# Batch 0 of an FFT filter with MLP: small columns on Pool, earlier angles, one filter copy and the last evacuation on ScalarE

## The chip, the cores and the metric

The kernel runs on one core of one Trainium2 chip. The metric is the device time of one execution in microseconds (us); lower is better. The kernel before took 772.74 us, the median of three runs from 772.51 to 773.15.

## The reference, cut to what matters

```python
X = np.fft.rfft(x, axis=1)                      # x: 8 batches x 3008 x 256
Y = X * (filt_r + 1j * filt_i)[None, :, :]      # 1505 frequencies x 256
y = np.fft.irfft(Y, n=3008, axis=1)
h = y.reshape(24064, 256) @ w_in                # 256 -> 2048
g = 0.5 * h * (1.0 + erf(h / sqrt(2)))
out = g @ w_out                                 # 2048 -> 256
```

## The kernel before

The sequence of 3008 is treated as 47 x 64. A first DFT stage (`c1`) works over 47 points, a second (`c2`) over 64, followed by the product with the filters; two inverse stages (`c3`, `c4`) give y_sb, which the MLP reads. The stages of batches 1 to 7 hide in the MLP of the batch before. Batch 0 has no MLP ahead of it, so it stands alone in the first 39 us, together with the building of the DFT tables. The change touches only that stretch. Pool issues all loads of x, filters and w_in in program order, one instruction each.

```python
def load_x(self, b, lo=0, n=32, hs=(0, 1)):
    ...
    for w in range(lo, lo + n, 8):
        for h in hs:
            nc.gpsimd.dma_start(out=xt[h * o:h * o + NA, w:w + 8, :], in_=xv[h][:, w:w + 8, :])

def load_filters(self, k0, k):
    for t, src in enumerate((self.filt_r, self.filt_i)):
        ...
        for q, a in enumerate((direct, mirror)):
            nc.gpsimd.dma_start(out=self.F[32 * q:32 * q + 32, t, k0:k0 + k, :], in_=a)

def dup_filters(self, eng, k0, k):          # filters land in 64 rows and are copied to the other 64
    for k in range(k0, k0 + k, 2):
        o, i = (self.F[r:r + 64, :, k:k + 2, :].rearrange("p t a b -> p t (a b)") for r in (64, 0))
        eng.tensor_copy(out=o, in_=i)
```

The start of the program, cut:

```python
m.load_x(0, 0, 8)                       # x loads 1, 2
m.k48 = m.iota(...)
m.load_x(0, 8, 8, (0,))                 # x load 3
m.kk = m.iota(...)
m.jj = ...                              # two iotas
m.load_x(0, 8, 8, (1,))                 # x load 4
cols = m.iota(...)
m.load_x(0, 16, 16)                     # x loads 5 to 8
...
m.table_1(g)                            # holds nine 128x1 columns that nobody needs yet
m.table_2_rows(g); ...; m.table_2_angle(g, 0); m.unit_matrices(g, cols)
for k, n in ((0, 4), (4, 8), (12, 12)):
    m.load_filters(k, n)                # three times four loads
m.load_w_in()
nc.gpsimd.memset(m.vt[:, :, 96, :], 0.0)
m.dup_filters(nc.gpsimd, 4, 20)
m.table_2_sin(0)
for u in range(16):
    m.c1(u // 2, u % 2, ...)            # L385: first DFT stage, four groups with table work between
    ...
m.table_3(1)
m.table_3_copy(1, False)
m.dup_filters(nc.vector, 0, 4)          # two filter copies on VectorE
m.c1t(0, (False, False)); m.c1t(1, (act,))
m.c2(0)                                 # L412: first filter product
m.table_3_turn(1)                       # the T3i turns, L256
m.c2(1)
...
        m.c4(u - 2, (act, False if u > 7 else act))   # last evacuation of y_sb on VectorE
```

## Time and profile before

| point of batch 0, kernel before | us |
|---|---|
| fourth group of L385 starts | 12.45 |
| last evacuation of the first stage (at_sb) on VectorE ends | 13.95 |
| first filter product (L412) starts | 15.82 |
| first Pool filter copy starts | 17.41 |
| last product (L417) ends | 30.08 |
| first matmul of the MLP (L482) starts | 38.76 |
| span ends | 770.6 |

Each row follows from the one above it on the same chain, but for the Pool copy, which feeds the third product. A microsecond saved matters only if it moves the row of 38.76. The prediction below shows the time line that these rows come from.

The time line columns are start us, length us, engine, line, operation and tiles, count, and in brackets the idle time and what ended it.

The second is the table of busy times by stretch, for the microsecond from 5.5 to 6.5. Its last two numbers are the share of time in which the DMA engines were busy (as the profile counts it, it can pass 1) and GB/s.

### The profile page before, as it was taken

To read this page: it belongs to the slowest core of one execution; us is meant where nothing else is said; L and a number is where in the kernel's file an instruction comes from. 1 tells how busy PE (TensorE), PEld (TensorE's weight loads), DVE (VectorE), ACT (ScalarE), POOL (GpSimd) and SP (SyncE) were. 2 spreads that over 40 slices of the span, in tenths; PEclk is the share of its full clock that TensorE was granted. 3 is DMA by queue.
4 is the path that set the end of the run, shared out by engine and by line. 5 is a ranking of instruction groups with operands and counts; after the bars stand their busy time and mean duration, and the time that the engine had idled before them with its cause. 6 is when DMAs were issued, how large, how long until landed. Compare 5 with 4: busy or idle time off the path is not lost.

```text
span 770.6 us, 15044 instructions
## 1 busy us (share of the span) xinstructions
PE 763.5 (99%) x6057; PEld 527.5 (68%) x6057; DVE 398.5 (52%) x737; ACT 566.7 (74%) x977; POOL 62.5 (8%) x154
## 2 busy tenths in 40 slices
PE   8999999999999999999999999999999999999998
PEld 5857666776766766677777777667676777766666
DVE  8957755564545645466463664627646366411011
ACT  6879855897568975699656996579865798666663
POOL 7701100010000200011000110001100000000000
PEclk9999999999999999999999999999999999999999
DMA  9884645366163661636526364345553422410111
GB/s 153 150 197 115 136 125 129 115 138 155 40 173 88 128 158 47 187 79 125 138 58 176 85 133 124 83 151 105 114 137 84 136 83 70 123 42 28 42 42 55
DMA packets 87270, 85.66 MB, mean 111 GB/s; under 512 B 6688, under 2 KB 77472, under 8 KB 87200
## 3 DMA queue, kind: packets, MB, share of 16 engines
q1 hardware_dynamic: 78816, 68.70, 31.3%
q0 software_dynamic: 8384, 16.00, 14.1%
q8 instruction: 47, 0.77, 0.4%
q14 instruction: 23, 0.19, 0.1%
HBM read 54.00 MB, written 46.66 MB: 131 GB/s over the span
## 4 chain that ended last, share of the span: by engine, by line
PE 94%; DMA 3%; POOL 2%; issue 0%; DVE 0%; POOLq 0%; SPq 0%
PE ps_o L509 43%; PE ps_h L482 42%; PE ps_s L369 2%; PE ps_s L344 2%; PE ps_s L319 2%; PE ps_s L296 2%; DMA x_sb<-in_x_dram 2%; POOL x_sb L83 1%; DMA F<-in_filt_i_dram 1%; POOL F L97 1%; DMA d_sb<-R 0%; POOL F L92 0%; PE ps_e L499 0%; POOL T1s L282 0%; DVE ost L522 0%
## 5 line engine op out<-in xcount | busy, mean ns | idle before, releaser
L485 ACT ACTIVATE g_sb<-ps_h 128x512 bf16<-128x512 f32 x752 | 438.0, 597 | 183.4 <-PE ps_h L482 172.6
L509 PE MATMUL ps_o<-w_out_sb,g_sb 128*128 128x256 bf16 x2992 | 447.5, 273 | 0.0
L482 PE MATMUL ps_h<-y_sb,w_in_sb 128*128 128x512 bf16 (+3 forms) x1600 | 445.8, 366 | 0.7 <-DMA x_sb<-in_x_dram 0.7
L509 PEld LDWEIGHTS <-g_sb 128*128 128x128 bf16 x2992 | 283.9, 98 | 134.3 <-issue 9.9
L482 PEld LDWEIGHTS <-w_in_sb 128*128 128x128 bf16 x1600 | 154.7, 98 | 23.7 <-issue 1.1
L515 DVE COPY ost<-ps_o 128x512 f32<-128x512 f32 x93 | 63.8, 686 | 143.5 <-PE ps_o L509 143.4
L327 DVE TENSOR_TENSOR p<-ps_s,F 128x512 bf16<-128x512 f32 x84 | 58.1, 692 | 105.8 <-ACT p L326 89.4
L273 DVE TENSOR_SCALAR y_sb<-ps_s 128x376 bf16<-128x376 f32 x112 | 61.0, 548 | 80.7 <-PE ps_s L369 80.7
L271 DVE CAST a_sb<-ps_s 128x512 bf16<-128x512 f32 x112 | 69.4, 683 | 27.7 <-PE ps_s L296 27.7
L271 DVE CAST v_sb<-ps_s 128x512 bf16<-128x512 f32 x84 | 57.4, 685 | 2.9 <-PE ps_s L344 2.9
L325 ACT ACTIVATE p<-ps_s 64x512 bf16<-64x512 f32 x84 | 49.8, 593 | 2.0
L326 ACT CAST p<-ps_s 64x512 bf16<-64x512 f32 x84 | 48.5, 577 | 1.0
L369 PEld LDWEIGHTS <-d_sb 96*128 96x128 bf16 x448 | 30.7, 97 | 25.6 <-DMA d_sb<-R 0.6
L102 POOL COPY gate<-p 1x1 bf16<-1x1 bf16 x48 | 8.5, 176 | 470.7 <-DVE p L329 470.7
L329 DVE TENSOR_TENSOR p<-p 128x512 bf16<-128x512 bf16 x84 | 35.7, 425 | 2.9
L369 PE MATMUL ps_s<-T,d_sb 96*128 96x94 bf16 x448 | 36.3, 204 | 0.1
L328 DVE TENSOR_TENSOR p<-p,F 128x512 bf16<-128x512 bf16 x84 | 34.9, 415 | 0.0
L83 POOL DMA_DIRECT2D x_sb<-in_x_dram x64 | 32.6, 511 | 13.3 <-issue 12.8
L344 PE MATMUL ps_s<-p,T 128*128 128x256 bf16 x168 | 32.1, 273 | 0.0
L319 PE MATMUL ps_s<-b_sb,T 128*128 128x256 bf16 x168 | 32.1, 273 | 0.0
L344 PEld LDWEIGHTS <-T 128*128 128x128 bf16 x168 | 16.4, 98 | 20.1 <-DVE p L329 0.5
L319 PEld LDWEIGHTS <-T 128*128 128x128 bf16 x168 | 16.4, 98 | 13.4
(113 smaller groups left out, 195.0 us busy)
## 6 DMA issues: line engine op xcount, KB each, us to landing
out_dram<-ost SPq DMA_DIRECT2D x93, 256.0 KB, 2.4
x_sb<-in_x_dram POOLq DMA_DIRECT2D x64, 188.0 KB, 3.6
R<-a_sb SPq DMA_DIRECT2D x112, 96.0 KB, 2.1
b_sb<-R SPq DMA_DIRECT2D x28, 384.0 KB, 4.1
R<-v_sb SPq DMA_DIRECT2D x42, 256.0 KB, 3.3
d_sb<-R SPq DMA_DIRECT2D x56, 192.0 KB, 4.7
w_in_sb<-in_moe_w_in_dram POOLq DMA_DIRECT2D x2, 512.0 KB, 9.0
w_out_sb<-in_moe_w_out_dram POOLq DMA_DIRECT2D x2, 512.0 KB, 11.0
```

Source lines behind the costliest of these rows:

```text
L271: self.nc.vector.tensor_copy(out=out, in_=in_)
L273: self.nc.vector.tensor_scalar(out=out, in0=in_, scalar1=scale, scalar2=None, op0=ALU.mult)
L319: nc.tensor.matmul(ps[:, 256 * i:256 * i + 256], lhsT=self.T2[:, k].rearrange("p a b -> p (a b)"), rhs=self.st[b, "b", k // 6][:, k % 6, : ...
L325: nc.scalar.activation(out=p2[0:64], in_=ps[64:128], func=AF.Copy, scale=-1.0)
L326: nc.scalar.copy(out=p2[64:128], in_=ps[0:64])
L327: nc.vector.tensor_tensor(out=p1, in0=ps, in1=f(0), op=ALU.mult)
L344: nc.tensor.matmul(ps[:, 256 * i:256 * i + 256], lhsT=self.T3[:, k].rearrange("p a b -> p (a b)"), rhs=w[:, 256 * i:256 * i + 256], start= ...
L369: nc.tensor.matmul(ps[:, 94 * i:94 * i + 94], lhsT=d[:, (grp % 2) * 4 + i, 128 * half:128 * half + 128], rhs=t4, start=True, stop=True)
L482: nc.tensor.matmul(ps[:, o:o + n], lhsT=self.w_in_sb[:, dc, jc * 128:jc * 128 + 128], rhs=self.ring[:, dc, off:off + n], start=(dc == 0), ...
L485: nc.scalar.activation(out=self.st["g", t][:, jc, :], in_=ps, func=AF.Gelu)
L509: nc.tensor.matmul(ps[:, tile_i % 2, :], lhsT=g[:, jc, tile_i * 128:tile_i * 128 + 128], rhs=self.w_out_sb[:, jc, :], start=(jc == 0), sto ...
L515: nc.vector.tensor_copy(out=ost, in_=ps)
```

## The change

It wants to shorten batch 0. Nine column operations leave VectorE's table work for Pool, where they stand one by one between the filter loads. The columns that the angles of table 2 need (table_2_rows) move ahead of the wide operations of table 1 on VectorE, and the copy T1c moves behind the first angle operation, so the angles start earlier; for this their iota (jj) is issued before the third x load. One of the two early filter copies goes to ScalarE, and so does the very last evacuation of y_sb.

```diff
-    def load_filters(self, k0, k):
+    def load_filters(self, k0, k, between=()):
...
                 nc.gpsimd.dma_start(out=self.F[32 * q:32 * q + 32, t, k0:k0 + k, :], in_=a)
+                next(between, None) if between else None
...
-            eng.tensor_copy(out=o, in_=i)
+            (eng.copy if eng is self.nc.scalar else eng.tensor_copy)(out=o, in_=i)
...
-        self.turn_signs(g)
-        self.weights_4(g)
+        self.table_2_rows(g)
...
+    def small_columns(self, g):
+        ts, tt = self.nc.gpsimd.tensor_scalar, self.nc.gpsimd.tensor_tensor
...
+        yield ts(out=self.wtc, in0=self.p, scalar1=4.0, scalar2=1.0, op0=ALU.is_ge, op1=ALU.add)
+        yield ts(out=q, in0=self.p, scalar1=64.0, scalar2=-64.0, op0=ALU.is_ge, op1=ALU.mult)
...        (seven more: q, b, turn_r, turn_i, q48 twice, wt)
...
-    m.load_x(0, 8, 8, (0,))
-    m.kk = m.iota(g, "kk", [128, 6], [[1, 6]])
     m.jj = g.tile([128, NB], FP32, name="jj")
...
-    m.load_x(0, 8, 8, (1,))
+    m.kk = m.iota(g, "kk", [128, 6], [[1, 6]])
+    m.load_x(0, 8, 8)
...
+    steps = m.small_columns(g)
     for k, n in ((0, 4), (4, 8), (12, 12)):
-        m.load_filters(k, n)
+        m.load_filters(k, n, steps)
...
+    m.dup_filters(nc.scalar, 0, 2)
     m.table_3_copy(1, False)
-    m.dup_filters(nc.vector, 0, 4)
+    m.dup_filters(nc.vector, 2, 2)
...
-            m.c4(u - 2, (act, False if u > 7 else act))
+            m.c4(u - 2, (False if u > 7 else act, act))
```

More of the change, by code (lines that the diff above doesn't have):

```diff
@@ L177, in table_2_angle @@
                                    in1=jn.unsqueeze(1).to_broadcast([128, 6, NB]), op0=ALU.mult, op1=ALU.add)
+            self.T1c = g.tile([2 * NA, 96], BF16, name="T1c")
+            v.tensor_copy(out=self.T1c.rearrange("p (k h r) -> p k h r", h=2, r=2),
+                          in_=self.T1.rearrange("p (h r k) -> p k h r", h=2, r=2))
             ts(out=w[:, 6:12], in0=w[:, 0:6], scalar1=n6, scalar2=None, op0=ALU.add)
@@ L183, in table_2_angle @@
            op0=ALU.logical_shift_left)
-    def turn_signs(self, g):
-        ts = self.nc.vector.tensor_scalar
-        q, b = (g.tile([128, 1], FP32, name=n) for n in ("q64", "b32"))
+    def small_columns(self, g):
+        ts, tt = self.nc.gpsimd.tensor_scalar, self.nc.gpsimd.tensor_tensor
+        q, b, r, self.wt, self.wtc = (g.tile([128, 1], FP32, name=n) for n in ("q64", "b32", "q48", "wt", "wtc"))
         self.turn = [g.tile([128, 1], FP32, name=n) for n in ("turn_r", "turn_i")]
-        ts(out=q, in0=self.p, scalar1=64.0, scalar2=-64.0, op0=ALU.is_ge, op1=ALU.mult)
-        self.nc.vector.tensor_tensor(out=q, in0=self.p, in1=q, op=ALU.add)
-        ts(out=b, in0=q, scalar1=32.0, scalar2=2.0, op0=ALU.is_ge, op1=ALU.mult)
-        ts(out=self.turn[0], in0=b, scalar1=1.0, scalar2=-1.0, op0=ALU.mult, op1=ALU.add)
-        ts(out=self.turn[1], in0=b, scalar1=-1.0, scalar2=1.0, op0=ALU.mult, op1=ALU.add)
+        yield ts(out=self.wtc, in0=self.p, scalar1=4.0, scalar2=1.0, op0=ALU.is_ge, op1=ALU.add)
+        yield ts(out=q, in0=self.p, scalar1=64.0, scalar2=-64.0, op0=ALU.is_ge, op1=ALU.mult)
+        yield tt(out=q, in0=self.p, in1=q, op=ALU.add)
+        yield ts(out=b, in0=q, scalar1=32.0, scalar2=2.0, op0=ALU.is_ge, op1=ALU.mult)
+        yield ts(out=self.turn[0], in0=b, scalar1=1.0, scalar2=-1.0, op0=ALU.mult, op1=ALU.add)
+        yield ts(out=self.turn[1], in0=b, scalar1=-1.0, scalar2=1.0, op0=ALU.mult, op1=ALU.add)
+        yield ts(out=r, in0=self.p, scalar1=48.0, scalar2=-48.0, op0=ALU.is_ge, op1=ALU.mult)
+        yield tt(out=r, in0=self.p, in1=r, op=ALU.add)
+        yield ts(out=self.wt, in0=r, scalar1=2.0, scalar2=1.0, op0=ALU.is_ge, op1=ALU.add)
     def unit_matrices(self, g, cols):
@@ L218, in table_2_swap @@
                        "act", 1.0 - 2.0 * i)
-    def weights_4(self, g):
-        ts = self.nc.vector.tensor_scalar
-        q, self.wt, self.wtc = (g.tile([128, 1], FP32, name=n) for n in ("q48", "wt", "wtc"))
-        ts(out=q, in0=self.p, scalar1=48.0, scalar2=-48.0, op0=ALU.is_ge, op1=ALU.mult)
-        self.nc.vector.tensor_tensor(out=q, in0=self.p, in1=q, op=ALU.add)
-        ts(out=self.wt, in0=q, scalar1=2.0, scalar2=1.0, op0=ALU.is_ge, op1=ALU.add)
-        ts(out=self.wtc, in0=self.p, scalar1=4.0, scalar2=1.0, op0=ALU.is_ge, op1=ALU.add)
     def table_4(self, t4, t1, wt, tag, eng):
@@ L563 @@
     m.table_1(g)
-    m.table_2_rows(g)
-    m.T1c = g.tile([2 * NA, 96], BF16, name="T1c")
-    nc.vector.tensor_copy(out=m.T1c.rearrange("p (k h r) -> p k h r", h=2, r=2),
-                          in_=m.T1.rearrange("p (h r k) -> p k h r", h=2, r=2))
     m.gen = m.py.tile([128, 2, K1, NB], FP32, tag="y", name="gen")
```

## The prediction

> **What bounds the kernel now.** I read three things in order: the busy table of the page, the time line of batch 0 (the first 39 us, the only part that the diff touches), and inside it what each engine waited for.
>
> ```profile
> PE 763.5 (99%) x6057; PEld 527.5 (68%) x6057; DVE 398.5 (52%) x737; ACT 566.7 (74%) x977; POOL 62.5 (8%) x154
> ```
>
> TensorE is busy for 99% of the span of 770.6 us. From 38.76 us on, when the first matmul of the MLP (L482) starts, it hardly pauses: the page shows 0.0 us of idle before L509 and 0.7 us before L482. So the last 732 us are a block of fixed length, and the change can only move its start. The time line of batch 0 says what sets that start; its columns are start us, length us, engine, line and tiles, count, and in brackets the idle time and what ended it.
>
> ```profile
> 8.61 0.72 PEld L385 LDWEIGHTS <-x_sb 94*128 94x128 bf16 x16 [0.64 <-issue]
> 8.79 0.55 POOL L92 DMA_DIRECT2D F<-in_filt_i_dram  x1 [0.53 <-DMA x_sb<-in_x_dram]
> ...
> 10.57 0.72 PEld L385 LDWEIGHTS <-x_sb 94*128 94x128 bf16 x16 [0.71 <-issue]
> 10.75 0.59 POOL L92 DMA_DIRECT2D F<-in_filt_r_dram  x1 [0.49 <-DMA x_sb<-in_x_dram]
> ...
> 12.45 0.72 PEld L385 LDWEIGHTS <-x_sb 94*128 94x128 bf16 x16 [0.41 <-issue]
> 12.63 0.58 POOL L92 DMA_DIRECT2D F<-in_filt_i_dram  x1 [0.30 <-DMA x_sb<-in_x_dram]
> ```
>
> The first DFT stage (L385) starts in four groups. In the program order each group waits for one pair of x loads, and each odd filter load on Pool waits for the second load of the same pair. Three times the weight load starts 0.18 us before the Pool load that the view says was released by x. "issue" only means that the view names no releaser; the equal lead says it was the landing of x, so the stage is paced by x at about 8.6, 10.6 and 12.4 us. The tables on VectorE and ScalarE do not pace it.
>
> ```profile
> 12.94 1.01 DVE L271 CAST at_sb<-ps_c 128x384 bf16<-128x384 f32 x2
> ...
> 13.99 0.90 DVE L97 COPY F<-F 64x1024 bf16<-64x1024 bf16 x2
> 14.01 1.07 PE L395 MATMUL ps_c1t<-eye,at_sb 128*128 128x128 bf16 x16
> ...
> 14.92 0.76 DVE L271 COPY b_sb<-ps_c1t 128x512 bf16<-128x512 bf16 x2
> 15.12 1.02 ACT L269 ACTIVATE b_sb<-ps_c1t 128x1024 bf16<-128x1024 bf16 x1 [0.28 <-PE ps_c1t L395]
> ...
> 15.82 1.23 DVE L412 TENSOR_TENSOR p<-ps_c,F 128x1024 bf16<-128x1024 f32 x1
> ...
> 17.41 9.90 POOL L97 COPY F<-F 64x1024 bf16<-64x1024 bf16 x10 [0.55 <-DMA F<-in_filt_i_dram]
> 17.48 11.40 DVE L412 TENSOR_TENSOR p<-ps_c,F 128x1024 bf16<-128x1024 f32 x10
> ```
>
> From 12.94 to 30.08 us VectorE is the bound: last evacuations of the DFT, two filter copies, two copies of b_sb, then the filter products (L412), ten of them 1.13 us apart (28.80 minus 17.48, over 10), then two halves to 30.08. Beside it Pool copies filters from 17.41 on, one per product. The rest of batch 0 follows from that end; its last lines are
>
> ```profile
> 32.92 5.48 ACT L269 ACTIVATE y_sb<-ps_c 128x376 bf16<-128x376 f32 x14 [0.60 <-ACT warm L640]
> ...
> 38.06 0.55 DVE L273 TENSOR_SCALAR y_sb<-ps_c 128x376 bf16<-128x376 f32 x1 [0.22 <-PE ps_c L459]
> 38.72 0.13 PEld L482 LDWEIGHTS <-w_in_sb 128*128 128x128 bf16 x2 [0.85 <-DMA x_sb<-in_x_dram]
> 38.76 0.59 PE L482 MATMUL ps_h<-y_sb,w_in_sb 128*128 128x512 bf16 x2 [0.73 <-DMA x_sb<-in_x_dram]
> ```
>
> The view puts the wait of L482 down to x. I do not believe it: L482 reads y_sb and w_in_sb, not x_sb. Its weight load waits for VectorE, which finished the last y_sb at 38.61 (38.06 + 0.55), 0.11 us before.
>
> **What the Trainium skill says.** "ScalarE: Activation LUTs", section "What ACT_TABLE_LOAD costs", gives 186 ns plus 0.833 ns per element and about 93 ns of overlap between neighbours: 1039 ns for 1024 elements, 946 ns apart. The trace has 1.02 us for a b_sb copy of that size, so it agrees. "GPSIMD Engine Reference", section "3.1 Elementwise — side-by-side cycle accounting", says that Pool passes an instruction through two software hops where VectorE has one; the trace shows the 1x1 gate copy on Pool at 176 ns and a 128x1 column on VectorE at about 150 ns, so a column costs about the same on either. "SBUF — State Buffer", section "Who interferes with whom", says that a VectorE copy or tensor_scalar in a 2-port mode and a Pool instruction exclude each other. The trace can't prove it, but the longest filter issue (0.70 us against a median of 0.57) is in the stretch at 14.3 us beside the two VectorE filter copies.
>
> **The change part by part.**
> - Nine column operations leave VectorE. In the time line they take from 1.86 to 3.06 us, 1.2 us. The angles also no longer stand behind the table-1 work, so I expect the last angle operation to end about 1 us earlier, at 5.6 in place of 6.68 us, and the first T2 sine (6.71) with it. On the path this is worth about 0: the groups at 8.6, 10.6 and 12.45 wait for x, and the x loads from the fifth on are issued after the same Pool work as before. At most T4c and the T3i turns (12.19 to 13.02) move up a little, which would let the evacuation at 12.94 start 0.1 us earlier.
> - The nine go to Pool between the filter loads, at an estimated 0.2 us each (from the 176 ns copy). The waits for x there are 0.38, 0.53, 0.43, 0.49, 0.49 and 0.30 us, so six fit into waits. The first stands after filter load 0, when transfers are still busy with x; the last two come after the waits and push the last four filter loads and w_in by about 0.4 us. Pool's memset ended at 16.86, and its first copy began at 17.41, so a slack of 0.55 us swallows that. Cost: 0.
> - One of the two early filter copies leaves VectorE: 0.45 us. The b_sb copy behind it needs eight transposes, ready about 14.6 us (14.01 plus the 0.61 us that a group of eight takes), so it starts at about 14.65 and not 14.92: 0.27 us. But the third product (L412) started at 18.61 and reads the filters of the first Pool copy, which ended at 18.46 (17.41 + 1.05) and was released by a filter transfer. Allowing 0.05 to 0.1 us for the signal, the product can start no earlier than 18.5. So of 0.27 (with the 0.1 above, 0.37) only about 0.1 us survives.
> - ScalarE gets that copy, about 0.95 us. It had 0.28 us idle before 15.12 and 0.56 before 16.70, together 0.84. The second b_sb ends at about 16.65 in place of 16.14, and its matmul also waits for the first product, which ends near 16.75. It just fits. Cost: 0.
> - The last y_sb goes to ScalarE: it starts at the same 38.06 when its matmuls end and takes 0.48 us in place of 0.55. Gain: 0.07 us. The VectorE half before it ends earlier.
>
> Sum: 0.1 + 0.07, about 0.2 us, and everything after it moves with it. 772.74 minus 0.2 is 772.5.
>
> **The rivals.**
> 1. The tables do pace batch 0, and the change gives what it seems to promise, some 0.5 to 1 us: 771.8 to 772.2. For it: VectorE is over 80% busy from the start, and ScalarE waited 2.3 us for the angles. Against it: the 0.18 us lead, three times.
> 2. Pool becomes the bound. If a column costs 0.3 us or more there, or is locked out by VectorE, filter loads are issued late, the first Pool copy starts after 17.41, and each 0.1 us of that passes to the products. Two to five tenths slower: 772.9 to 773.2. For it: the slack on Pool is only 0.55 us and the wait before load seven 0.30.
> 3. The filter transfer that releases Pool's first copy lands earlier, since four later loads compete with it 0.4 us later. Then the cap at 18.5 lifts, and the full 0.4 us come through: 772.3. I have no number against it, so I lean a little that way within the range.
> 4. ScalarE becomes the bound near 16.7 us, if its copy takes over 1.1 us: the chain loses its gain, 772.7.
>
> **Range and chances.** All mechanisms lie between 1 us faster and 0.5 us slower. Three runs of before spread by 0.64 us (772.51 to 773.15), as much as any of these effects. So 771.8 to 773.1 should hold it 8 times in 10. Two per cent would be 15.5 us, 40% of the whole of batch 0; I give 1% to either side and 98% to the same.
>
> **What would show it.** Right: the L385 groups start at about 8.6, 10.6 and 12.45 us as before while the first T2 sine is near 5.7; the first Pool copy of F starts near 17.4; the third L412 at about 18.5 and directly behind that copy; the first L482 at 38.5 to 38.6. Wrong: the L385 groups move up with the sine (rival 1); Pool's first copy moves late, or early (rivals 2 and 3); the second b_sb copy holds up TensorE near 16.8 (rival 4); or the MLP's length of 732 us changes by more than the move of its start, which would mean that I was wrong to treat it as a block.

## More of the kernel before

```profile
2.59 0.21 POOL L121 IOTA k<- 128x48 f32 x1
2.73 0.52 POOL L83 DMA_DIRECT2D x_sb<-in_x_dram  x1
3.25 0.18 POOL L121 IOTA kk<- 128x6 f32 x1
3.36 0.29 POOL L555 IOTA jj<- 128x32 f32 x2
3.57 0.52 POOL L83 DMA_DIRECT2D x_sb<-in_x_dram  x1
4.09 0.26 POOL L121 IOTA cols<- 128x128 f32 x1
4.27 2.02 POOL L83 DMA_DIRECT2D x_sb<-in_x_dram  x4
```

The third x load goes out at 2.73, ahead of kk and jj, and the fourth at 3.57, behind them.

```profile
core 0: us, PE busy (x) PEld busy (x) DVE busy (x) ACT busy (x) POOL busy (x), PEclk, DMA share, GB/s
5.50:6.50 1.00, 0.98 (x9) 0.61 (x9) 0.93 (x3) 0.00 (x0) 1.00 (x3) 1.00 1.03 168
```

The transfers are busy without a gap here.

## The result, and the profile after

The changed kernel took 773.39 us, the median of six runs from 772.75 to 775.45. The kernel before, run beside it, had 773.08 over six runs. The ratio is 1.001, with a 95% interval of 0.9997 to 1.0023. A ratio here is always the mean time of one kernel's fast runs over the mean of the other's of the same rounds, so it is not quite the ratio of the medians that are quoted. By the 2% measure the two are the same, as I expected; but I had expected a gain of 0.2 us and a time of at most 773.1, and both failed. All outputs are right.

The busy table of the changed kernel answers to the first line in the prediction.

```profile
PE 763.0 (99%) x6057; PEld 526.9 (68%) x6057; DVE 397.2 (51%) x727; ACT 568.1 (74%) x978; POOL 65.2 (8%) x163
```

Ten instructions left VectorE, nine came to Pool and one to ScalarE. The nine columns, 2.17 us together, are most of Pool's extra 2.7 us.

The time line of batch 0 of the changed kernel, with the lines that answer to those of before:

```profile
2.75 0.30 POOL L553 IOTA jj<- 128x32 f32 x2
2.98 0.19 POOL L122 IOTA kk<- 128x6 f32 x1
3.08 1.04 POOL L83 DMA_DIRECT2D x_sb<-in_x_dram  x2
...
5.74 0.84 ACT L217 ACTIVATE T<-gen 128x768 bf16<-128x768 int32 x1 [1.55 <-DVE gen L186]
...
9.03 0.72 PEld L385 LDWEIGHTS <-x_sb 94*128 94x128 bf16 x16 [1.62 <-issue]
9.21 0.63 POOL L92 DMA_DIRECT2D F<-in_filt_i_dram  x1
...
12.77 0.60 PEld L385 LDWEIGHTS <-x_sb 94*128 94x128 bf16 x13 [0.29 <-issue]
...
13.44 1.01 DVE L271 CAST at_sb<-ps_c 128x384 bf16<-128x384 f32 x2
...
14.40 1.04 ACT L98 COPY F<-F 64x1024 bf16<-64x1024 bf16 x1
14.48 0.42 DVE L98 COPY F<-F 64x1024 bf16<-64x1024 bf16 x1
15.17 0.75 DVE L271 COPY b_sb<-ps_c1t 128x512 bf16<-128x512 bf16 x2 [0.26 <-PE ps_c1t L395]
16.13 1.22 DVE L412 TENSOR_TENSOR p<-ps_c,F 128x1024 bf16<-128x1024 f32 x1 [0.21 <-PE ps_c L408]
...
18.17 3.97 POOL L98 COPY F<-F 64x1024 bf16<-64x1024 bf16 x4 [0.47 <-DMA F<-in_filt_i_dram]
19.24 10.28 DVE L412 TENSOR_TENSOR p<-ps_c,F 128x1024 bf16<-128x1024 f32 x9 [0.23 <-POOL F L98]
...
39.04 0.28 PEld L482 LDWEIGHTS <-w_in_sb 128*128 128x128 bf16 x2 [0.53 <-DMA x_sb<-in_x_dram]
39.23 0.59 PE L482 MATMUL ps_h<-y_sb,w_in_sb 128*128 128x512 bf16 x2 [0.57 <-DMA x_sb<-in_x_dram]
```

The first sine (T) came 0.97 us earlier than the 6.71 of before, yet the group of L385 that had started at 8.61 now starts at 9.03, and the one at 12.45 at 12.77. Behind its one filter copy VectorE now waits for transposes, then turns the first product out 1.68 us after the last at_sb (14.45 to 16.13; before 13.95 to 15.82, 1.87). Then the third product waits 0.23 us for Pool's filter copy, which itself waited for a filter transfer and began 0.76 us later than before. The first MLP matmul is at 39.23 instead of 38.76.

The same stretch of the windows as before:

```profile
core 0: us, PE busy (x) PEld busy (x) DVE busy (x) ACT busy (x) POOL busy (x), PEclk, DMA share, GB/s
5.50:6.50 1.00, 0.51 (x13) 0.54 (x14) 0.86 (x5) 0.76 (x2) 1.00 (x3) 1.00 0.78 119
```

The transfers seem to have a gap here: a share of 0.78 against 1.03. The third x load was issued at 3.08 instead of 2.73. This gave the theory to test: the change's order of x loads makes x land later, which costs more than the other parts gain. The rivals were that Pool's columns push the filter loads, and that all of it is the spread between runs.

### The profile page after: what moved, and what is told of

It reads as the page before. It is cut to its first block, busy times and chain, and to the rows that moved or that the text cites. A ratio compares the mean times of both kernels' runs of the same rounds, so it can differ in the third digit from the quotient of the medians.

```text
span 771.7 us, 15048 instructions
## 1 busy us (share of the span) xinstructions
PE 763.0 (99%) x6057; PEld 526.9 (68%) x6057; DVE 397.2 (51%) x727; ACT 568.1 (74%) x978; POOL 65.2 (8%) x163
## 4 chain that ended last, share of the span: by engine, by line
PE 93%; DMA 3%; DVE 2%; POOL 1%; ACT 1%; issue 0%; SPq 0%; DVEq 0%; POOLq 0%
PE ps_o L509 42%; PE ps_h L482 41%; PE ps_s L369 2%; PE ps_s L344 2%; PE ps_s L319 2%; PE ps_s L296 2%; DMA x_sb<-in_x_dram 1%; DMA d_sb<-R 1%; POOL F L98 1%; DMA R<-a_sb 1%; POOL x_sb L83 1%; DMA R<-v_sb 1%; DVE a_sb L271 0%; PE ps_e L499 0%; ACT T L269 0%
## 5 line engine op out<-in xcount | busy, mean ns | idle before, releaser
L482 PE MATMUL ps_h<-y_sb,w_in_sb 128*128 128x512 bf16 (+3 forms) x1600 | 446.0, 366 | 0.6 <-DMA x_sb<-in_x_dram 0.6
L482 PEld LDWEIGHTS <-w_in_sb 128*128 128x128 bf16 x1600 | 154.8, 98 | 23.8 <-issue 1.4
```

Of the source, the lines that this page charges most:

```text
L482: nc.tensor.matmul(ps[:, o:o + n], lhsT=self.w_in_sb[:, dc, jc * 128:jc * 128 + 128], rhs=self.ring[:, dc, off:off + n], start=(dc == 0), ...
```

## The experiments

Sixteen runs followed, in groups, each group on one chip and beside runs of the kernel before. I read every profile at five points that add up to the start of the MLP: the fourth group of L385 ("group 4"), from there to the end of the last at_sb, on to the first product, through the products, and from the end of the products to the first L482. "A" is the changed kernel, "B" the kernel before.

### How far the same kernel differs from itself: b_again, a_again, a_third, a4, a5

No edit: B once more and A four times more.

> The kernel before, unchanged, to see how far two executions of one kernel differ. If the 0.47 us by which the changed kernel's first L482 came later (39.23 against 38.76) is a real shift, this one starts L482 within 0.15 us of 38.76, has the second L385 group at 8.5 to 8.7, Pool's first F copy at 17.3 to 17.5, and a time ratio of 1.000. If the shift was jitter of the transfers (rival), these points spread by 0.3 to 0.5 us here too.

> The changed kernel, unchanged. Real shift: first L482 within 0.15 us of 39.23, second L385 group near 9.03, first F copy near 18.17, ratio 1.0003 to 1.001. Jitter: L482 anywhere from 38.6 to 39.3, and the groups move with it.

> The changed kernel a third time. Two of its profiles put the fourth L385 group at 12.77 and 13.51, five with the old order of x loads and no Pool column at 12.43 to 12.82. If the change delays x: 12.8 or later again, L482 at 39.2 or later, and its times stay about 0.5 us over those of the kernel before. If it is jitter: 12.4 to 12.7 is as likely. In either case the products' end to L482 takes 8.5 us and the last at_sb to the first product 1.68.

> The changed kernel again, beside the same kernel with only the old order of iotas and x loads (ai2, ai3). If the new order delays x: fourth L385 group at 12.8 or later here and at 12.2 to 12.7 in ai2 and ai3, and the pooled times about 0.4 us apart. If the earlier spread was jitter: the two kinds overlap, with means within 0.2 us.

> The changed kernel again, a second time in this call. Order theory: fourth L385 group at 12.8 or later; jitter: it overlaps with ai2 and ai3.

Measured: b_again 773.48 us (ratio 1.0004); a_again 773.42, a_third 773.37, a4 773.49, a5 773.42 (ratios 1.0004, 1.0005, 1.0005, 1.0001, each with an interval of about 0.0013 to either side). No single ratio leaves the noise. In the profiles group 4 of A started at 12.77, 13.51, 12.96, 12.54 and 13.17, and of B at 12.45 and 12.65. The first L482 was at 39.20 to 39.68 in A's five, and at 38.76 and 39.02 in B's two. The stretch from there to the end was 731.80 to 732.54 us in A and 731.84 and 732.38 in B.

What follows: the stretch behind the first L482 alone varies by 0.7 us with no edit at all, and B's two profiles differ by 0.26 us before it, so an effect of 0.3 us needs many runs. Taking all runs on all chips together, B has 51 of them with a median of 773.13 and a mean of 773.12 (standard error 0.08, range 772.08 to 774.88), and A has 26 with a median of 773.42 and a mean of 773.51 (0.13). So A is some 0.3 to 0.4 us slower.

### The order of x loads: a_iota_back, ai2, ai3 undo it; b_iota does it alone

The edit of the first three, from A, each the same kernel; b_iota is the reverse, from B:

```diff
+    m.load_x(0, 8, 8, (0,))
+    m.kk = m.iota(g, "kk", [128, 6], [[1, 6]])
     m.jj = ...
-    m.kk = m.iota(g, "kk", [128, 6], [[1, 6]])
-    m.load_x(0, 8, 8)
+    m.load_x(0, 8, 8, (1,))
```

> The changed kernel with the old order of iotas and x loads. Theory X: groups back at 8.6, 10.6 and 12.45, and L482 0.3 us or more earlier than in the changed kernel, at 38.7 to 38.9; whatever is left against 38.6 is Pool's columns. Rival L: groups stay at 9.0 and 12.8.

> The changed kernel with the old order of iotas and x loads. Order theory: fourth group 12.2 to 12.7, L482 at 38.4 to 38.8 if the products do not wait, share of the transfers in 5.5 to 6.5 us at 0.9 or more (0.75 to 0.79 in three of the profiles with the new order). Jitter: as a4.

> The changed kernel with the old order of iotas and x loads, a second time in this call. Order theory: fourth L385 group at 12.2 to 12.7; jitter: it overlaps with a4 and a5.

> The kernel before with only the order of the iotas and of the third and fourth x load changed (kk and jj ahead of both). Theory X: this delays the third x load by 0.35 us, leaves the transfers a gap, and x lands 0.3 to 0.4 us later: second L385 group near 9.0, fourth near 12.8, F copy near 17.7 to 18.1, L482 near 39.1. Rival L (the earlier angles on VectorE block Pool while it writes descriptors): as before, groups at 8.6 and 12.45, L482 near 38.76.

Measured: a_iota_back 772.74, ai2 773.17 and ai3 772.89 us (ratios 0.9998, 1.0001, 0.9997). Their 16 runs have a mean of 773.04 (standard error 0.16), 0.47 below A's 773.51, with a standard error of the difference of 0.21. Their group 4 started at 12.43, 12.04 and 12.51, mean 12.33, against A's mean of 12.99, Pool's first copy at 17.35, 17.30 and 17.71 against 18.00 to 18.63 in A, and the MLP at 38.55, 39.16 and 39.12 against 39.20 to 39.68. In the group of runs made for this question (a4 and a5 beside ai2 and ai3) the means were 773.30 and 773.01, only 0.29 apart, with a standard error of 0.19. The rival in the expectations, that VectorE's earlier angles hold Pool up while it issues, would have left a_iota_back's groups at 9.0 and 12.8; they were at 8.62 and 12.43.

Two runs told below make a second pair that differs in this order alone, with the columns on VectorE: a_cols_dve (new order) has group 4 at 13.24 and a mean time of 773.19 us, best (old order) 12.19 and 772.90. With a_cols_x4, at 12.52, the seven profiles of the changed kernel and its variants with the new order lie from 12.52 to 13.51, and the four with the old order from 12.04 to 12.51.

The DMA share from 5.5 to 6.5 us was 0.96 to 1.06 in the three with the order undone, and 0.75, 0.75, 0.78, 0.87 and 0.98 in A. But the gap and the delay do not go together: a4, with 0.75, has A's earliest group 4 (12.54), while a_again, with 0.98, and a_cols_dve, with 1.03, have the latest (13.51 and 13.24). And b_cols, with the old order, also has 0.87.

b_iota took 773.54 (ratio 1.0002), much as b_again's 773.48, with group 4 at 12.72 and a share of 0.99: no gap. Its group 4 lies among those of the old order in B's program: 12.45 and 12.65 in B, 12.82 and 12.81 in b_evac and b_fcopy, whose edits come later in the program. Its MLP did start late, at 39.22, but after a wait of the filter products and not of x. From its time line:

```profile
22.53 5.95 POOL L97 COPY F<-F 64x1024 bf16<-64x1024 bf16 x6 [0.97 <-DMA F<-in_filt_i_dram]
23.60 5.75 DVE L412 TENSOR_TENSOR p<-ps_c,F 128x1024 bf16<-128x1024 f32 x5 [0.24 <-POOL F L97]
...
39.22 0.59 PE L482 MATMUL ps_h<-y_sb,w_in_sb 128*128 128x512 bf16 x2 [0.73 <-DMA x_sb<-in_x_dram]
```

What follows: in the changed kernel undoing this one line of the order gives back about 0.45 us in both times and profiles, and the columns stay on Pool in that comparison. In the kernel before the same order moves x by nothing that stands out of the spread in its one profile. So the order is the best supported cause, not a proven one: it shows in A against its undoing, where neither the first Pool copies nor the starts of group 4 overlap, the latter by a bare 0.03 us (12.51 and 12.54). By what way it delays x is not shown.

Of these, ai2 also shows why an early x is not passed on in full. From its time line, Pool and VectorE:

```profile
17.06 5.93 DVE L412 TENSOR_TENSOR p<-ps_c,F 128x1024 bf16<-128x1024 f32 x5
17.30 3.97 POOL L98 COPY F<-F 64x1024 bf16<-64x1024 bf16 x4 [0.34 <-DMA F<-in_filt_i_dram]
22.64 2.98 POOL L98 COPY F<-F 64x1024 bf16<-64x1024 bf16 x3 [1.36 <-DMA F<-in_filt_i_dram]
23.70 5.75 DVE L412 TENSOR_TENSOR p<-ps_c,F 128x1024 bf16<-128x1024 f32 x5 [0.71 <-POOL F L98]
```

After four copies Pool waits 1.36 us for the next filter transfer, and the seventh product waits 0.71 us for the copy. The products took 15.24 us here, against 14.26 in B's first profile, and the MLP started at 39.16, although group 4 had been 0.41 us earlier than in B.

### The last evacuation alone: b_evac

```diff
-            m.c4(u - 2, (act, False if u > 7 else act))
+            m.c4(u - 2, (False if u > 7 else act, act))
```

> The kernel before with the last two y_sb evacuations swapped and nothing else. In the profiles so far the last evacuation ended 0.15 us before L482 where VectorE did it (38.61 and 38.76) and 0.06 us before where ScalarE did it (39.17 and 39.23). Theory: the last weight load no longer waits, so from the last d_sb copy to L482 it saves 0.15 to 0.2 us, not the 0.07 that I predicted. Rival: only the 0.07. The landing of x is as in the kernel before (fourth L385 group 12.4 to 12.7).

Measured: 772.87 us, ratio 1.0004. From the end of the products to the first L482 it took 8.52 us, against 8.68 and 8.69 in B's profiles, and 8.51 or 8.52 in every kernel with this edit. The time line of b_evac:

```profile
37.67 1.06 DVE L273 TENSOR_SCALAR y_sb<-ps_c 128x376 bf16<-128x376 f32 x2
38.85 0.28 PEld L482 LDWEIGHTS <-w_in_sb 128*128 128x128 bf16 x2 [0.53 <-DMA x_sb<-in_x_dram]
39.04 0.59 PE L482 MATMUL ps_h<-y_sb,w_in_sb 128*128 128x512 bf16 x2 [0.57 <-ACT y_sb L269]
```

What follows: the gain on the path is 0.17 us. The weight load now starts 0.19 us ahead of its matmul, where before it was 0.04 us ahead (38.72 and 38.76): it waits no longer for the last evacuation, only the matmul does. In the time of whole runs 0.17 us is not to be seen.

### One filter copy on ScalarE alone: b_fcopy

```diff
+    m.dup_filters(nc.scalar, 0, 2)
     m.table_3_copy(1, False)
-    m.dup_filters(nc.vector, 0, 4)
+    m.dup_filters(nc.vector, 2, 2)
```

> The kernel before with one of the two early filter copies on ScalarE and nothing else. Theory: from the end of the last at_sb evacuation to the first product (L412) the time falls from 1.87 us (13.95 to 15.82) to about 1.65, but the third product then waits for Pool's first F copy, and at most 0.1 us is left there. Rival: the first product does not come earlier, since ScalarE's T3 and b_sb copies run late. L482 within 0.15 us of the fourth L385 group plus 26.3.

Measured: 773.01 us, ratio 1.0001. The last at_sb to the first product took 1.68 us, against 1.87 and 1.82 in B's two profiles: a gain of 0.14 to 0.19. The products took 14.74 us, against 14.26 and 14.25: a loss of 0.5. Pool's first copy came at 18.31, though nothing of Pool's work had been changed; it had waited 1.22 us for a filter transfer (0.55 in B), and a product waited 0.4 us for it; the MLP started at 39.52. So the gain is real and local, and in this one profile a later landing of filters takes it away.

### The columns: b_cols moves them alone, a_cols_dve keeps them on VectorE, a_cols_x4 multiplies them

b_cols takes the nine columns from VectorE's table 1 in B and puts them between the filter loads on Pool. a_cols_dve is A with them on VectorE behind the unit matrices. a_cols_x4 is A with three copies of each column ahead of it, into a scratch column:

```diff
-        yield ts(out=self.wtc, in0=self.p, ...)
+        ts(out=z, in0=self.p, ...)          # three times, and so for all nine
+        yield ts(out=self.wtc, in0=self.p, ...)
```

> The kernel before with the nine columns on Pool between the filter loads; old order of x loads and of VectorE's tables. Theory: a column costs 0.2 to 0.25 us on Pool, the eighth filter load is still issued 0.18 us after the fourth L385 group, the last four come 0.4 to 0.8 us later after it than before (twelfth load then about 3 us after the eighth, before 2.35). Rival X2: the x landing also moves (fourth group at 12.8 or later)[...]. First F copy 4.9 us after the eighth load as before if the columns do not slow that transfer.

> The changed kernel with the nine columns back on VectorE, behind the unit matrices, none on Pool. If Pool's columns cost the changed kernel its gain: L482 at the fourth L385 group plus 26.0 to 26.1, time 0.2 to 0.4 us under the changed kernel. If the new order of x loads costs it: the fourth group stays at 12.8 or later. If it is jitter alone: the fourth group anywhere from 12.4 to 13.5, and the ratio within 1.0000 plus or minus 0.0010.

> The changed kernel with every Pool column done four times (three into a scratch column), a dose of some 27 columns at 0.2 to 0.25 us more. Theory that Pool's place between the waits matters: the eighth filter load falls behind the fourth L385 group by 2 us or more in place of 0.18, the first F copy comes 3 to 6 us later, and L482 is at 41 to 45, time up by 2 to 6 us. Rival (the waits for x and the queue of transfers hide it): L482 under 40. Results stay right.

Measured: b_cols 773.11 us (ratio 0.9999), a_cols_dve 773.10 (1.0002), a_cols_x4 778.91 (1.0074, from 1.0061 to 1.0088). A column took 0.19 to 0.25 us on Pool, but 0.41 to 0.75 where it ran beside a VectorE tensor_scalar or filter copy (0.75 in a_iota_back, beside the two T3i turns). With 27 extra columns the w_in issue moved from 16.36 in A to 22.63, the first Pool copy to 23.96, and the MLP's start to 45.02. The waits of a_cols_x4 in batch 0 (engine, line, releaser: us in total, times, longest; its L439 is the product and L283 the turn):

```profile
DVE p L439 <- POOL F L98: 2.0, 1, 2.0
DVE T3i L283 <- POOL turn_r L214: 2.0, 1, 2.0
...
DVE T3i L283 <- POOL turn_i L218: 1.2, 1, 1.2
```

What follows: rival 2 of my prediction describes a true mechanism, and Pool has room for nine columns but not for 36. With nine, moving them either way is not seen in the time. The profiles are less clear. In b_cols, with group 4 at 12.61 as in B, the last pair of filter loads went out at 15.26 (14.30 in B), Pool waited 1.18 us for a filter transfer before its fifth copy, the products took 15.05 us and the MLP started at 39.69. In a_cols_dve, without columns on Pool, it started even later, at 39.93: group 4 stayed late at 13.24, as its expectation said if the order costs, and Pool waited 1.46 us before its fifth copy. b_cols had its first copy at 17.85, inside the range of B, b_again, b_evac and b_fcopy, which have none there (17.41 to 18.31), and the three profiles with the order of x undone had theirs at 17.30 to 17.71 with all nine columns on Pool.

### All x loads earlier: b_x_first

```diff
-    m.load_x(0, 0, 8)
+    m.load_x(0, 0, 16)
...
-    m.load_x(0, 8, 8, (0,))
...
-    m.load_x(0, 8, 8, (1,))
```

> The kernel before with the third and fourth x loads issued directly behind the first two and the iotas after them. If issue order paces x: the second group comes 0.3 to 0.5 us earlier (8.1 to 8.3) and the fourth too (12.0 to 12.2), though the first sine is later, at 7.5 to 7.9. If the rate of the transfers paces x: the fourth group stays at 12.4 to 12.8.

Measured: 774.57 us, ratio 1.0018, from 1.0005 to 1.0031: slower. The transfers ran at 209 GB/s from 5.5 to 6.5 us and the eighth filter load, which had been behind x by my reading, went out at 12.09 (12.63 in B). But the iotas came later, the first sine at 7.46, and group 4 started at 12.74. The MLP started at 40.57: from group 4 to the last at_sb it took 2.07 us (1.50 and 1.61 in B), and the products took 15.30, with the two turns stretched as in best below. So x and the tables are close behind each other: early x with late tables is no gain, as A showed for the reverse.

### A version to beat both: best

A with the columns on VectorE behind the unit matrices (as in a_cols_dve) and the old order of x loads.

> The changed kernel with the old order of x loads and the columns on VectorE behind the unit matrices: it keeps the earlier angles, the filter copy on ScalarE and the swapped last evacuation. At_sb to first product 1.68 us and products' end to L482 8.5 us, so 0.3 us less than the kernel before in the fixed steps; L482 at the fourth group plus 26.0 to 26.1 when the products do not wait for filters. Time 0.3 us under the kernel before, which five rounds can't tell from nothing.

Measured: 772.85 us, ratio 0.9997, from 0.9985 to 1.001. Group 4 started at 12.19, the first Pool copy at 16.32, and yet the MLP at 39.56. VectorE's time line of best:

```profile
15.80 1.23 DVE L412 TENSOR_TENSOR p<-ps_c,F 128x1024 bf16<-128x1024 f32 x1 [0.21 <-PE ps_c L408]
16.95 0.56 DVE L256 TENSOR_SCALAR T3i<-T,turn_r 128x512 bf16<-128x512 bf16 x1
17.43 1.12 DVE L256 TENSOR_SCALAR T3i<-T,turn_i 128x512 bf16<-128x512 bf16 x1
18.47 2.33 DVE L412 TENSOR_TENSOR p<-ps_c,F 128x1024 bf16<-128x1024 f32 x2
```

The two turns took 0.56 and 1.12 us; in B they took 0.35 each, and Pool's first copy began at 17.41, when the second was half done. Here Pool copies from 16.32 on, about 1.03 us a copy, and the second turn lasts about as long as one. The Trainium skill, "SBUF — State Buffer", section "Who interferes with whom", says that a tensor_scalar in a two-port mode and a Pool instruction exclude each other for the whole length of either; these lengths agree with it, as do the 0.62 and 1.12 us of the turns in b_x_first, whose first copy was at 16.18. The second product started at 18.47, where undisturbed turns would have let it start at about 17.47, my estimate (16.95 plus 0.52 us, as from 16.96 to 17.48 in B). Best is not shown to beat B.

## Why the prediction was right or wrong

The mean of each point over the profiles, two of B, five of A, three of A with the order of x undone (us):

| part | B | A | order undone |
|---|---|---|---|
| start of group 4 | 12.55 | 12.99 | 12.33 |
| to the end of the last at_sb | 1.56 | 1.55 | 1.61 |
| to the first product | 1.85 | 1.68 | 1.68 |
| the products | 14.26 | 14.66 | 14.81 |
| to the first L482 | 8.69 | 8.52 | 8.52 |
| sum: first L482 | 38.89 | 39.40 | 38.94 |

A against the undoing differs by 0.46 us in the sum, and by 0.47 in the mean time of 26 and 16 runs. A against B differs by 0.51 in the sum and by 0.39 in the time of 26 and 51 runs. B's first row is the least sure: with b_evac and b_fcopy, which run B's program up to there, its mean is 12.68, and A's delay of 0.44 us becomes 0.31.

1. **The bound.** Right. TensorE was 99% busy in both, and the change can only move the start of the MLP.
2. **The MLP as a block of fixed length, and the noise.** This step failed. I took three runs within 0.64 us for the spread. The block of 732 us is 731.66 to 732.64 in the profiles, and 51 runs of B have a median of 773.13, above the top of my range: even without any effect a run would have missed it as often as not.
3. **The x loads cost nothing.** The failed step in the mechanism. I wrote that "the x loads from the fifth on are issued after the same Pool work as before". That is nearly true (4.27 and 4.31), and beside the point: the third was issued 0.35 us later (2.73 to 3.08). I had myself read that x paces the groups, and then did not ask what the change does to x. The table puts about 0.66 us on it between A and the undoing. How the late issue delays x is not shown: a gap in the transfers from 5.5 to 6.5 us does not go with the delay, and b_iota shows neither.
4. **The earlier sine is worth nothing on the path.** It came at 5.74, predicted near 5.7, and A's groups did not move up with it, so rival 1's gain of 0.5 to 1 us never came. In the undoing group 4 was 0.2 us earlier than in B; with best, four profiles with the early sine and the old order have it at 12.04 to 12.51, and five with the later sine and that order (B's two, b_evac, b_fcopy, b_cols) at 12.45 to 12.82. So a gain of up to 0.4 us is possible, where I had 0 to 0.1; no run moves the sine alone.
5. **The columns on Pool.** The estimate of 0.2 us each held (0.19 to 0.25). I expected w_in 0.4 us later; it was 0.77 (15.59 to 16.36), of which I put 0.32 on x, by which group 4 moved, and the remaining 0.45 on the columns. Pool's slack of 0.55 us did not "swallow" that in A, since the first copy was 0.76 us late; but with the order undone it began at 17.45 in the mean, where B's two have 17.54. So the columns alone do not make it late. But they have a share that the runs do not separate: in a_again, a_third and a5 the view names no transfer before the first copy, so Pool's own work set it, and in a_again that copy capped the products. Rival 2 came nearest in size; the runs with the order undone speak against it as the main reason.
6. **The filter copy.** Right in kind, wrong in size: the step to the first product gained 0.17 us in the mean, not 0.27, since b_sb waited for the transposes and the product then for its matmul (0.26 and 0.21 us in the time line of A). The cap at the third product was there as written, directly behind Pool's first copy. I had left 0.1 us of the gain; in fact nothing was left, because the copy came later.
7. **The second wait for filters.** Missing from the prediction. I treated only the first Pool copy as a cap. The next transfer also holds Pool, by 0.22 us in A's first profile, 0.43 in b_again, 0.70 in a_iota_back and 1.36 in ai2, and the products took 14.66 us in A against 14.26 in B. This is most of why 0.66 us at group 4 were only 0.46 at the end. Fifteen of the 18 profiles fall into three kinds, by what the end of the products follows at a fixed distance: the first product, by 14.25 or 14.26 us (B, b_again, b_evac); Pool's first copy, by 12.53 or 12.54 (A's first, a_again, a4, b_fcopy); or its fifth copy, by 8.00 to 8.02 (a_third, a5, the three with the order undone, b_iota, b_cols, a_cols_dve). So no profile of A ends at VectorE's own pace, and in the third kind an earlier x helps only if the last filter transfer also lands earlier.
8. **Rival 3, filters landing earlier free the full 0.4 us.** The runs speak against it. In A the copy came later, not earlier. In best and b_x_first it was at 16.32 and 16.18, and the turns of T3i were stretched beside it by about 1 us in all.
9. **ScalarE.** Its copy took 1.04 us against an estimate of 0.95, and b_sb behind it held nothing up: the second product came 1.67 us after the first, as in B (1.66). Rival 4 did not happen.
10. **The last evacuation.** Right in sign, mis-sized: the term of 0.07 measured 0.17. I counted only the shorter evacuation. In B the first matmul came 0.15 us after the evacuation's end (38.61 to 38.76), in A 0.06 (39.17 to 39.23), since the weights were loaded already.

The expected 0.2 us is there, even more: 0.17 for the copy and 0.17 for the evacuation. It went to a later landing of x and to waits for filters. What stays open: by what way the order of issue delays x and why b_iota shows no such delay, what share the columns have, why the transfers' rate varies between profiles of one kernel, and how much of the length of the products (14.25 to 15.30 us over all profiles but that of a_cols_x4) is the kernel's and how much chance.

## What to carry to other kernels

Where a landing paces a stage, every instruction moved ahead of its issue has to be costed, however small: check the issue times of all loads in the changed program order, not only those of the last. Work taken off the chain's engine pays only up to the next wait, so follow the chain past the first cap to the next transfers. And for an effect of some tenths of a microsecond, measure the unchanged kernel against itself first; three runs do not give its spread.

## What the Trainium skill lacked or had wrong

- "GPSIMD Engine Reference", section "3.1 Elementwise — side-by-side cycle accounting", speaks of long operations; it has no cost of a 128x1 column on Pool. The runs show 0.19 to 0.25 us on Pool, and 0.41 to 0.75 beside a VectorE tensor_scalar or filter copy, against 0.13 to 0.16 on VectorE.
- No page that I read gives a spread of landing of the same loads. Five profiles of one kernel had the group that waits for the last x pair at 12.54 to 13.51 us.
- None has the lag from an evacuation to the matmul that reads it: 0.15 us where the weight load waited as well, 0.06 where only the matmul did.
